# The last slice of the last tile scaled on the scalar engine and stored from its own queue, the slice ahead of it on VectorE

## The chip, the cores and the metric

The kernel runs on one core of a Trainium2 chip. The metric is the device time of one execution in microseconds.

Some terms: a *semaphore* is a counter by which engines and stores tell each other that something is done, and an *event* is a moment at which one is raised. A store is *issued* from the queue of an engine, which is held meanwhile; in the traces it then raises its semaphore sixteen times, and the last of these events is its *landing*. The *exit* is what the program still does after the last landing.

## The reference, cut to what matters

Spatially reduced attention over 4 x 12288 queries of 128 channels is followed by a gated feed-forward network with 1536 hidden channels.

```python
def _moe_ref(x, w_gate, w_val, w_out):
    gate = np.maximum(x @ w_gate, 0.0)
    val = x @ w_val
    return (gate * val @ w_out).astype(np.float32)     # 49152 rows of 128 channels
```

The rows are worked off in 96 tiles of 512. The change touches the last of them alone, after its last matrix product: the values lie in PSUM, have to be multiplied by a constant, and have to be stored to memory.

## The kernel before

```python
    def out_scale(k, engine, own, o_ps=None):
        ...                                  # o_sb: three buffers used in turn
        if engine is nc.scalar:
            nc.scalar.mul(o_sb, o_ps, 1.0 / X_SCALE**2)
        else:
            nc.vector.tensor_scalar(o_sb, o_ps, 1.0 / X_SCALE**2, None, op0=ALU.mult)

    def out_store(k, own):
        nc.sync.dma_start(out[...][:, own], o_sbs[k][:, own])     # address cut

    def out_last(k):
        parts = [bank([128, 2, 128]), bank([128, 1, 128]), bank([128, 1, 128])]
        owns = [slice(0, 2), slice(2, 3), slice(3, 4)]
        ...
        def keep(n, engine):
            out_scale(k, engine, owns[n], parts[n])
            out_store(k, owns[n])
        held = NFB - 1
        add(0, 0, held)                       # add: matmuls of one slice of 128 rows
        add(1, 0, held)
        add(2, 0, held - 4)
        add(0, held, NFB)
        add(1, held, NFB)
        keep(0, nc.vector)                    # slices 0 and 1
        add(2, held - 4, NFB)
        keep(1, nc.scalar)                    # slice 2
        add(3, 0, NFB)
        keep(2, nc.vector)                    # slice 3: the last work of the kernel
```

In the main loop, the last two tiles ahead of this one are stored whole, also from the sync queue: `out_scale(kO, nc.vector, slice(0, NS)); out_store(kO, slice(0, NS))` and the same on ScalarE just before `out_last`.

The softmax here doesn't subtract the row's maximum and nothing guards it: scores larger than these inputs give would overflow.

Of the kernel before, what the change touches and what calls it, by code (L numbers as in the profile page):

```python
# [16 lines left out]
def kernel(  # L17
# [23 lines left out]
    nc = tc.nc  # L41
# [27 lines left out]
    def bank(shape, dtype=FP32):  # L69
        return psum.tile(shape, dtype, tag="bank", name="bank_ps")  # L70
# [228 lines left out]
    def out_add(k, fb, s, o_ps, first):  # L299
        nc.tensor.matmul(  # L300
            o_ps, hTs[k][:, fb, s * 128 : (s + 1) * 128], wo16[:, fb, :],
            start=first, stop=(fb == NFB - 1), skip_group_check=True,
        )
# [44 lines left out]
    def out_scale(k, engine, own, o_ps=None):  # L348
        if k not in o_sbs:
            o_sbs[k] = work.tile([128, NS, 128], FP32, tag="o_sb", bufs=3, name="o_sb")  # L350
        o_sb, o_ps = o_sbs[k][:, own], o_ps if o_ps is not None else o_banks[k]
        if engine is nc.scalar:
            nc.scalar.mul(o_sb, o_ps, 1.0 / X_SCALE**2)
        else:
            nc.vector.tensor_scalar(o_sb, o_ps, 1.0 / X_SCALE**2, None, op0=ALU.mult)

    def out_store(k, own):
        nc.sync.dma_start(
            out[k // GRP * GRP * T : (k // GRP + 1) * GRP * T, :].rearrange(
                "(p i s) c -> i p s c", p=128, i=GRP  # L360
            )[k % GRP][:, own], o_sbs[k][:, own],
        )
        if own.stop == NS:
            for tiles in (hTs, o_banks, o_sbs):
                del tiles[k]
# [4 lines that stand above are left out]
        o_banks[k] = None  # L370

        def add(s, fb0, fb1):
            n = max(s - 1, 0)
            for fb in range(fb0, fb1):
                out_add(k, fb, s, parts[n][:, s - owns[n].start], fb == 0 and s != 1)

        def keep(n, engine):
            out_scale(k, engine, owns[n], parts[n])
            out_store(k, owns[n])

        held = NFB - 1
        add(0, 0, held)
# [3 lines that stand above are left out]
        add(1, held, NFB)  # L386
        keep(0, nc.vector)
        add(2, held - 4, NFB)
        keep(1, nc.scalar)
        add(3, 0, NFB)  # L390
        keep(2, nc.vector)

    ctx.enter_context(tc.manual_schedule())

# [138 lines left out]
    for k in range(LAG, last + 1):  # L533
# [6 lines left out]
        for step in range(NFB):  # L540
            kO, kF = k - LAG - 1, k - LAG
            half, i = divmod(step // 2, NJC // 2)
            if 0 <= kO:
                out_proj(kO, step)
                if step == NFB - 1 and kO < NT - 3:
                    out_moves = out_turn(kO)
                elif step == NFB - 1 and k < last:
                    out_scale(kO, nc.vector, slice(0, NS))
                    out_store(kO, slice(0, NS))
# [41 lines left out]
            if b < B:  # L591
# [13 lines left out]
                if 0 <= pair < NJC // 2 and not odd and step == 1:  # L605
                    turn_values_dma(b, pair)
    out_scale(last - LAG - 1, nc.scalar, slice(0, NS))
    out_store(last - LAG - 1, slice(0, NS))
    out_last(last - LAG)


# [28 lines left out]
```

## Time and profile before

| | |
|---|---|
| time, median of the 6 runs beside the result | 1033.86 us (1033.05 to 1034.48) |
| span in the profile | 1031.32 us |
| TensorE busy | 1023.6 us, 99% |
| last matmul's semaphore event | 1027.94 us |
| **tail: from that event to the end of the span** | **3.379 us** |

The lines behind this are in the prediction. The tail is the quantity to follow: all that the change touches lies in it or just ahead of it. It is made of five steps, each read from the trace's records to the nanosecond: the event to the start of the last scale, the scale, its end to the start of the store's issue, issue to the last landing event, and from there to the end.

### The profile page before, as it was taken

What the parts mean: (1) busy time and instruction counts of PE and PEld (TensorE: products, weight loads), DVE (VectorE), ACT (ScalarE), POOL (GpSimd) and SP (SyncE); (2) the same over time, 40 slices, a digit from 0 to 9 for tenths busy, and PEclk for the clock granted to TensorE, in tenths of its full rate; (3) what the DMA queues carried; (4) which work ended last, traced back from release to release, by engine and by line L of the source; (5) the groups of instructions that cost most, each with busy time, mean ns of one, the idle gap of its engine ahead of it and who ended that gap; (6) DMA issues with size and microseconds to landing.
All of it is one profiled execution on the core that took longest, in us unless ns stands there. A gap on an engine that the chain in (4) does not pass through costs nothing.

```text
span 1031.3 us, 20034 instructions
## 1 busy us (share of the span) xinstructions
PE 1023.6 (99%) x6576; PEld 545.2 (53%) x6576; DVE 910.4 (88%) x1669; ACT 909.6 (88%) x1749; POOL 279.9 (27%) x287
## 2 busy tenths in 40 slices
PE   8999999999999999999999999999999999999998
PEld 5555555555555555555555555555555555555555
DVE  3889899998989898998889898989898888989898
ACT  4998888888988888888888889888888898888886
POOL 2212146521211124642212121664121221111110
PEclk9999999999999999999999999999999999999999
DMA  8836396452542547736345157573752434513122
GB/s 306 121 57 81 90 192 142 79 93 43 83 68 49 79 120 161 169 54 89 55 65 88 32 85 148 137 170 57 85 75 44 73 57 62 87 32 66 33 44 51
DMA packets 328824, 93.34 MB, mean 91 GB/s; under 512 B 308496, under 2 KB 321936, under 8 KB 328720
## 3 DMA queue, kind: packets, MB, share of 16 engines
q1 hardware_dynamic: 313632, 78.76, 38.7%
q0 software_dynamic: 14944, 13.24, 10.5%
q8 instruction: 51, 0.84, 0.3%
q14 instruction: 53, 0.43, 0.1%
q10 hardware_dynamic: 144, 0.07, 0.0%
HBM read 53.94 MB, written 26.35 MB: 78 GB/s over the span
## 4 chain that ended last, share of the span: by engine, by line
PE 98%; DMA 1%; ACT 0%; DVE 0%; SPq 0%; issue 0%
PE bank_ps L279 24%; PE bank_ps L290 24%; PE bank_ps L314 23%; PE bank_ps L241 13%; PE bank_ps L230 12%; DMA parts<-in_kv_dram 1%; PE bank_ps L300 1%; PE bank_ps L163 0%; PE bank_ps L189 0%; ACT aT L231 0%; DVE hT L293 0%; PE bank_ps L181 0%; SPq L139 0%; ACT kv L183 0%; PE bank_ps L119 0%
## 5 line engine op out<-in xcount | busy, mean ns | idle before, releaser
L293 DVE SCALAR_TENSOR_TENSOR hT<-bank_ps,val 128x512 f16<-128x512 f32 x1152 | 758.2, 687 | 91.6 <-ACT val L283 71.1
L283 ACT CAST val<-bank_ps 128x512 f16<-128x512 f32 x1152 | 678.7, 591 | 102.5 <-PE bank_ps L279 100.5
L279 PE MATMUL bank_ps<-xT,wv 128*128 128x512 f16 x1152 | 436.6, 379 | 0.1
L290 PE MATMUL bank_ps<-xT,wg 128*128 128x512 f16 x1152 | 436.6, 379 | 0.0
L314 PE MATMUL bank_ps<-hT,wo 128*128 128x512 f16 x1116 | 423.0, 379 | 0.0
L231 ACT ACTIVATE aT<-bank_ps 128x512 f16<-128x512 f32 x576 | 346.3, 605 | 0.9 <-PE bank_ps L230 0.8
L324 POOL TENSOR_SCALAR o_sb<-o_t 128x512 f32<-128x512 f32 x93 | 138.5, 1489 | 694.0 <-DVE rinv L249 684.1
L241 PEld LDWEIGHTS <-aT 128*128 128x128 f16 x2304 | 177.2, 98 | 133.4 <-issue 0.9
L241 PE MATMUL bank_ps<-kv,aT 128*128 128x129 f16 x2304 | 223.5, 220 | 0.5 <-DVE kv L199 0.4
L230 PE MATMUL bank_ps<-qT,kv 128*128 128x512 f16 x576 | 216.8, 379 | 0.4 <-DVE qT L122 0.2
L279 PEld LDWEIGHTS <-wv 128*128 128x128 f16 x1152 | 112.7, 98 | 132.2 <-issue 0.2
L290 PEld LDWEIGHTS <-wg 128*128 128x128 f16 x1152 | 112.7, 98 | 67.2 <-issue 0.2
L314 PEld LDWEIGHTS <-wo 128*128 128x128 f16 x1116 | 109.2, 98 | 65.9
L230 PEld LDWEIGHTS <-kv 128*128 128x128 f16 x576 | 56.1, 98 | 68.0 <-ACT kv L183 0.8
L257 DVE TENSOR_TENSOR x<-bank_ps,rinv 128x256 f16<-128x256 f32 x188 | 79.7, 425 | 6.6
L322 DVE STREAM_TRANSPOSE o_t<-bank_ps 128x512 f32<-128x512 f32 x93 | 65.7, 706 | 0.0
L86 POOL DMA_DIRECT2D q<-in_q_dram x88 | 48.4, 557 | 0.3 <-issue 0.3
L148 POOL TENSOR_TENSOR s<-parts 128x512 f32<-128x512 f32 x36 | 44.9, 1267 | 0.0
L249 DVE RECIPROCAL rinv<-bank_ps 128x2 f32<-128x2 f32 x192 | 28.0, 146 | 0.6 <-PE bank_ps L241 0.6
L150 POOL TENSOR_TENSOR s<-s 128x512 f32<-128x512 f32 x18 | 22.8, 1269 | 1.4
L152 POOL TENSOR_TENSOR c<-s 128x256 f32<-128x256 f32 x18 | 13.1, 728 | 1.4
L300 PEld LDWEIGHTS <-hT 128*128 128x128 f16 x144 | 10.1, 98 | 6.1 <-DVE hT L293 0.3
(53 smaller groups left out, 95.0 us busy)
## 6 DMA issues: line engine op xcount, KB each, us to landing
parts<-in_kv_dram SPq DMA_DIRECT2D x48, 512.0 KB, 6.6
out_dram<-o_sb SPq DMA_DIRECT2D x354, 64.0 KB, 2.2
q<-in_q_dram POOLq DMA_DIRECT2D x88, 128.0 KB, 4.4
xT<-x SPq DMA_TRANSPOSE x94, 2.5
out_dram<-o_sb SPq DMA_DIRECT2D x80, 16.0 KB, 1.5
placed<-blocks SPq DMA_DIRECT2D x9, 128.0 KB, 1.8
kvT<-placed SPq DMA_DIRECT2D x36, 32.0 KB, 2.0
q<-in_q_dram SPq DMA_DIRECT2D x2, 512.0 KB, 7.9
```

Source lines behind the costliest of these rows:

```text
L86: nc.gpsimd.dma_start(q16[32 * j : 32 * (j + 1)].rearrange("t (i s) c -> t i s c", i=GRP), rows[j])
L230: nc.tensor.matmul(s_ps, kv16[:, k // NST, jc, 0:C], qT_of(k), start=True, stop=True)
L231: nc.scalar.activation(aTs[k][:, jc, :], s_ps, AF.Exp, scale=qk_scale)
L241: nc.tensor.matmul(x_ps[:, i, :], aTs[k][:, jc, s * 128 : (s + 1) * 128], kv16[:, k // NST, jc, C : 2 * C + 1], start=(jc == 0 and i == 0) ...
L257: nc.vector.tensor_tensor(x16s[k][:, 2 * half : 2 * half + 2, :], x_ps[:, :, 0:C], rinv.to_broadcast([128, 2, C]), op=ALU.mult,)
L279: nc.tensor.matmul(va_ps, wv16[:, fb * 128 : (fb + 1) * 128], xTs[k], start=True, stop=True)
L283: nc.scalar.copy(val, va_ps)
L290: nc.tensor.matmul(g_ps, wg16[:, fb * 128 : (fb + 1) * 128], xTs[k], start=True, stop=True)
L293: nc.vector.scalar_tensor_tensor(hTs[k][:, fb, :], g_ps, 0.0, vals.pop((k, fb)), op0=ALU.max, op1=ALU.mult)
L314: nc.tensor.matmul(o_banks[k], wo16[:, fb, :], hTs[k][:, fb, :], start=fb == 0, stop=fb == NFB - 1)
L322: nc.vector.transpose(o_t, o_banks.pop(k))
L324: nc.gpsimd.tensor_scalar(o_sb.rearrange("t j s c -> t s j c"), o_t.rearrange("t (s j c) -> t s j c", s=NS, j=4), 1.0 / X_SCALE**2, None, ...
```

## The change

The intent is to give the last store an empty queue: the engine that scales the last slice also issues its store, and does not stand behind the two sync stores ahead. The slice ahead then goes to VectorE.

```diff
-    def out_store(k, own):
-        nc.sync.dma_start(
+    def out_store(k, own, queue=nc.sync):
+        queue.dma_start(
...
-        def keep(n, engine):
+        def keep(n, engine, queue=nc.sync):
             out_scale(k, engine, owns[n], parts[n])
-            out_store(k, owns[n])
+            out_store(k, owns[n], queue)
...
-        keep(1, nc.scalar)
+        keep(1, nc.vector)
         add(3, 0, NFB)
-        keep(2, nc.vector)
+        keep(2, nc.scalar, nc.scalar)
```

## The prediction

> **What bounds the kernel now.** I read the page first, for which engine fills the span and whether the end of the kernel can matter at all.
>
> ```profile
> span 1031.3 us, 20034 instructions
> PE 1023.6 (99%) x6576; PEld 545.2 (53%) x6576; DVE 910.4 (88%) x1669; ACT 909.6 (88%) x1749; POOL 279.9 (27%) x287
> PE 98%; DMA 1%; ACT 0%; DVE 0%; SPq 0%; issue 0%
> ```
>
> TensorE fills 99% of the span and 98% of the chain that ended last. The change touches no matmul. So whatever it does happens in the few microseconds after the last matmul. The chain in order of time, asked for the last 7 us, shows where that tail begins:
>
> ```profile
> 1025.63 2.31 PE bank_ps L300 x38
> 1027.94 0.02 issue
> 1027.96 0.29 DVE o_sb L355
> ```
>
> The last matmul releases VectorE at 1027.94. From there to the end of the span, 1031.3, are 3.36 us, 0.33% of the span. Even if all of it vanished, the result would be "within 2%". What is left to find is the sign and the tenths of a microsecond. The timeline of the tail, engine by engine (columns: start in us, duration in us, engine, line, operation):
>
> ```profile
> 1027.34 0.28 ACT L353 ACTIVATE o_sb<-bank_ps 128x128 f32<-128x128 f32 x1 [1.49 <-PE bank_ps L300]
> ...
> 1027.07 0.42 DVE L355 TENSOR_SCALAR o_sb<-bank_ps 128x256 f32<-128x256 f32 x1 [0.90 <-PE bank_ps L300]
> 1027.96 0.29 DVE L355 TENSOR_SCALAR o_sb<-bank_ps 128x128 f32<-128x128 f32 x1 [0.47 <-PE bank_ps L300]
> ...
> 1027.53 0.33 SPq L358 DMA_DIRECT2D out_dram<-o_sb  x1
> ...
> 1027.95 0.39 SPq L358 DMA_DIRECT2D out_dram<-o_sb  x1
> ...
> 1028.43 0.40 SPq L358 DMA_DIRECT2D out_dram<-o_sb  x1
> ```
>
> Three pieces of the last tile are scaled (slices 0-1 on VectorE, slice 2 on ScalarE, slice 3 on VectorE), and three stores leave one after another from the sync queue. The last scale ends at 1027.965 + 0.292 = 1028.257 (the trace's records to the ns), yet its store starts only at 1028.429. It waits for its queue, not for its data. The second store is issued until 1028.337, and a semaphore instruction stands between the two (1028.383, 17 ns). Where the queue was free, for the first store, the start came 28 ns after the scale's end (1027.499 to 1027.527). So 172 - 28 = 144 ns of the path to the end is the sync queue's own issuing. That is what the change can win.
>
> After the issue, the line's own view and the queue's waits give the rest:
>
> ```profile
> L358 SPq DMA_DIRECT2D out_dram<-o_sb x1: 397/397/397, 1028.4 to 1028.4; - x1
> DMA to landing us min/median/max: 1.7/1.7/1.7
> ...
> SPq L635 <- DMA out_dram<-o_sb: 1.1, 3, 0.5
> ```
>
> The last landing event is at 1030.150, 1.721 us after the issue began, and the exit (sync's remaining checks, then two rounds of all engines) runs to 1031.32, 1.17 us more. The wait at L635 is sync waiting for the last three landings in turn.
>
> **What the Trainium skill says.**
> 1. "DMA: Bandwidth & Descriptors", section "Issuing engines are not separate DMA queues": stores from different engines share the same 16 DMA engines, and issuing from several saves only the sequencer's issue time. The trace agrees that this time is what is at stake: an issue holds sync 0.33 to 0.40 us, the landing takes 1.7 to 1.9.
> 2. "Perfetto Trace Analysis", section "DMA Instruction — HWDGE (DVE, Sync)": the block that generates descriptors is shared between issuing sequencers and locked for one at a time. The trace has one hint: at the start, the one load from ScalarE's queue (0.732, 377 ns) lay beside the first load from sync (0.729), whose issue took 696 ns against about 600 for the next ones. That suggests sharing at a cost of some 0.1 us, not a full wait.
> 3. "ScalarE: Activation LUTs", section "What ACT_TABLE_LOAD costs": an ACTIVATE with immediate scale takes 186 ns plus 0.833 ns per element, so 293 ns at 128. The trace has 278 for just this shape, which I use.
>
> **The change, part by part.**
>
> *Slice 2 moves from ScalarE to VectorE.* It needs the matmuls of slice 2 (ScalarE began at 1027.343) and VectorE free of the first piece (1027.499). It runs about 1027.50 to 1027.50 + 0.29 = 1027.79, against 1027.62 now, 0.17 later. Its store cannot be issued by sync before 1027.952 in either kernel, since the first store holds the queue to 1027.859 and the semaphore instruction and dispatch add 93 ns. Slack 0.16 us; cost on the path: zero.
>
> *Slice 3 moves from VectorE to ScalarE.* The matmul's semaphore event is at 1027.941. VectorE started 24 ns after it because its older waits were already met. ScalarE in the present kernel started 72 ns after its event (1027.271 to 1027.343), because its wait is split: semaphore instructions ahead, then the operation. Those waits, on the earlier stores of the buffer, go with the first use of the new tile by an engine, so they will stand ahead of ScalarE's slice 3 too. Start 1027.941 + 0.072 = 1028.013. End + 0.278 = 1028.291, 34 ns later than VectorE's 1028.257 (48 lost at the start, 14 won in duration).
>
> *The last store moves to ScalarE's queue.* It is the only store there, so it starts about 28 ns after the scale: 1028.32 instead of 1028.429, which is 0.11 earlier. Sync issues the second store until 1028.337, so the two hardly overlap (about 20 ns). Landing: 1.72 us as now, or 1.79 as ScalarE's own load of the same 64 KB at the start (0.732 to its last landing event, 2.517):
>
> ```profile
> 0.73 0.38 ACTq L403 DMA_DIRECT2D w_sr_f<-in_w_sr_dram  x1
> ...
> w_sr_f<-in_w_sr_dram ACTq DMA_DIRECT2D x1, 64.0 KB, 1.8
> ```
>
> That gives 1030.04 to 1030.11 against 1030.150: a gain of 0.04 to 0.11 us.
>
> *The exit.* The semaphores of stores go round in program order over both queues (the trace shows the same one for ScalarE's load and for later sync stores). The last store therefore should keep its place in sync's list of final waits, and the exit its 1.17 us. The second store lands at 1029.758 as now, before the last one, so it does not become the end. ScalarE's closing drain comes earlier than sync's.
>
> Sum: 0.00 (slice 2) + 0.034 (slower start on ScalarE) - 0.144 (no queue ahead) + 0 to 0.07 (landing) = -0.11 to -0.04 us. The span goes from 1031.3 to about 1031.2, and the time from 1033.97 to 1033.9.
>
> **The rivals.**
>
> *The shared descriptor block makes the store from ScalarE wait or slows it.* For it: the skill's statement, and the 0.1 us longer issue of the first load. Also, first packets moved 0.997 us after the ScalarE issue began, against some 0.89 for the last sync stores (1028.429 to 1029.320). Against it: the overlap here is only about 20 ns. If the whole 0.1 applies, the gain is zero: 1033.95 to 1034.05.
>
> *The exit order changes.* If the new store were waited for last rather than in the middle, sync's four checks after it (each about 60 ns apart, 1030.167 to 1030.408) would be done before the landing, and another 0.2 us would go: 1033.65. Against it: the semaphores rotate as said. If ScalarE's queue brings one more check or drain: plus 0.06 to 0.1, 1034.0.
>
> *ScalarE is late for another reason.* Its waits on nine store semaphores could be met late. Against it: in the present kernel they run at 1024.8 to 1025.4 and the last stands idle for 1895 ns. The buffer's old stores have long landed. At most a tenth of a microsecond.
>
> **Range and chances.** All of these together span 1033.6 to 1034.1. The three runs before spread over 1033.8 to 1034.48, so run-to-run variation is larger than the whole effect. I widen to 1033.1 to 1034.6 for it and for another session. The middle is 1033.9. Reaching 2% would take 20.7 us, six times the whole tail: 0.99 within, half a per cent on either side for an accident I cannot see.
>
> **What would show it right or wrong.** Right: slice 2 on VectorE directly behind the first piece with the second sync issue still near 10 ns of its place relative to the last matmul; slice 3 on ScalarE starting some 70 ns after the last matmul's event and lasting 0.28; a store on ScalarE's queue starting about 0.38 us after that event (sync: 0.49 now); landing 1.7 to 1.8 us later; an exit of 1.17 us. Wrong steps: a second sync store that starts later; a ScalarE issue much over 0.40 us or a landing over 1.85 (contention); an exit of another length (wait order). The prediction itself would be wrong if the main loop moved, that is, if the last matmul's event shifted by microseconds, which nothing in this change should cause.

## The result, and the profile after

The changed kernel took 1033.53 us, median of 6 runs (1032.74 to 1034.25), against 1033.86 before. The ratio is 0.9997 with a 95% interval of 0.9984 to 1.001: the same. (A ratio is the mean time of one kernel's fast runs over that of the other's of the same rounds, so not quite the ratio of the medians quoted.) The times alone do not show that anything changed.

The profile does. First the page of the changed kernel:

```profile
span 1031.8 us, 20033 instructions
PE 1023.4 (99%) x6576; PEld 544.4 (53%) x6576; DVE 909.9 (88%) x1669; ACT 909.6 (88%) x1749; POOL 279.9 (27%) x287
PE 97%; DMA 1%; ACT 1%; DVE 0%; SPq 0%; issue 0%; ACTq 0%
```

The span of this one execution is 0.44 us longer than the one of before, although the changed part became shorter. The chain of the tail in order of time shows both:

```profile
1026.14 2.31 PE bank_ps L300 x38
1028.45 0.03 ACTq L353
1028.48 0.04 issue
1028.53 0.28 ACT o_sb L353
```

The last matmul's event came at 1028.454, 0.513 us later than in the profile before, because of work that the change does not touch (see "How much the rest of the kernel moves"). From there the chain goes to ScalarE now. The timeline of the changed kernel (start, duration, engine, line, operation):

```profile
1027.59 0.42 DVE L355 TENSOR_SCALAR o_sb<-bank_ps 128x256 f32<-128x256 f32 x1 [0.90 <-PE bank_ps L300]
1027.93 0.28 DVE L355 TENSOR_SCALAR o_sb<-bank_ps 128x128 f32<-128x128 f32 x1
...
1028.53 0.28 ACT L353 ACTIVATE o_sb<-bank_ps 128x128 f32<-128x128 f32 x1 [2.15 <-PE bank_ps L300]
1028.83 0.35 ACTq L358 DMA_DIRECT2D out_dram<-o_sb  x1
...
1028.04 0.33 SPq L358 DMA_DIRECT2D out_dram<-o_sb  x1
...
1028.46 0.38 SPq L358 DMA_DIRECT2D out_dram<-o_sb  x1
```

VectorE scales slice 2 directly behind the first piece; ScalarE scales slice 3 and issues its store 29 ns after the scale's end. Its issue overlaps that of the second sync store by 15 ns (1028.833 to 1028.848). What follows the issue:

```profile
L358 ACTq DMA_DIRECT2D out_dram<-o_sb x1: 353/353/353, 1028.8 to 1028.8; - x1
DMA to landing us min/median/max: 1.8/1.8/1.8
...
SPq L635 <- DMA out_dram<-o_sb: 1.5, 3, 1.0
```

The third line, from the queue's waits, was 1.1 us in total with 0.5 as the longest before: sync has one store less to issue, stands at its closing checks earlier and waits longer there. Longer waiting on an engine that has nothing else to do is not a loss. The five steps side by side, in ns:

| step | before | predicted | after | difference |
|---|---|---|---|---|
| event to scale | 24 | 72 | 72 | +48 |
| scale | 292 | 278 | 278 | -14 |
| scale to issue | 172 | 28 | 29 | -143 |
| issue to last landing | 1721 | 1721 to 1790 | 1753 | +32 |
| landing to end | 1170 | 1170 | 1170 | 0 |
| **tail** | **3379** | | **3302** | **-77** |

### The profile page after: what moved, and what is told of

Same layout as the page of the kernel before. It is cut to its first block, busy times and chain, and to the rows that moved or that the text cites. A ratio compares the mean times of both kernels' runs of the same rounds, so it can differ in the third digit from the quotient of the medians.

```text
span 1031.8 us, 20033 instructions
## 1 busy us (share of the span) xinstructions
PE 1023.4 (99%) x6576; PEld 544.4 (53%) x6576; DVE 909.9 (88%) x1669; ACT 909.6 (88%) x1749; POOL 279.9 (27%) x287
## 4 chain that ended last, share of the span: by engine, by line
PE 97%; DMA 1%; ACT 1%; DVE 0%; SPq 0%; issue 0%; ACTq 0%
PE bank_ps L279 24%; PE bank_ps L290 24%; PE bank_ps L314 23%; PE bank_ps L241 13%; PE bank_ps L230 12%; DMA xT<-x 1%; DMA parts<-in_kv_dram 1%; PE bank_ps L300 1%; PE bank_ps L163 0%; ACT aT L231 0%; PE bank_ps L189 0%; DVE hT L293 0%; PE bank_ps L181 0%; SPq L139 0%; ACT kv L183 0%
```

## The experiments

The theory: the gain is the sync queue's issue time, no longer in front of the last store. The exchange of engines gains nothing and costs the 48 ns at ScalarE's start. The rival: the exchange of engines is what helps. A second rival is chance. Nine kernels ran; all gave correct results. Each was profiled, and this is what the traces' records say, in ns after the last matmul's event (its place in the span, in us, is in the second column). "Store ahead" is the last landing event of the store before the last.

| run | event, us | scale start | scale end | issue | store ahead landed | landed | tail |
|---|---|---|---|---|---|---|---|
| before | 1027.94 | 24 | 316 | 488 | 1817 | 2209 | 3379 |
| r_before | 1028.23 | 22 | 314 | 486 | 1806 | 2206 | 3376 |
| after | 1028.45 | 72 | 350 | 379 | 1801 | 2132 | 3302 |
| r_after | 1029.33 | 72 | 350 | 380 | 1800 | 2128 | 3298 |
| e1_swap_only | 1028.20 | 72 | 349 | 488 | 1790 | 2213 | 3383 |
| e2_queue_only | 1029.03 | 22 | 314 | 346 | 1801 | 2116 | 3286 |
| e3_both_scalar | 1028.60 | 23 | 300 | 330 | 1815 | 2116 | 3286 |
| e4_middle_store | 1028.09 | 23 | 314 | 342 | 1831 | 2081 | 3251 |
| e5_both_scalar_queue | 1028.33 | 23 | 315 | 347 | 1833 | 2088 | 3258 |
| e6_later_check | 1027.99 | 71 | 348 | 378 | 1885 | 2109 | 3037 |
| e7_middle_and_check | 1028.08 | 23 | 314 | 342 | 1895 | 2107 | 3036 |

### r_before and r_after: does the tail repeat?

No edit; the two kernels again.

> The kernel before, unchanged, profiled once more. Theory: the tail, from the last matmul's semaphore event to the end of the span, is fixed by instructions and transfers (3.379 us in the first profile) and repeats to about 0.02 us, while the event itself moves between executions by some tenths of a microsecond (1027.94 in the first profile of before, 1028.45 in that of after). Rival: the tail itself varies by as much as the 0.077 us between the two first profiles (3.379 and 3.302), and that difference says nothing.

> The changed kernel, profiled once more. Theory: tail 3.30 us within 0.02, made of 0.072 to the scale, 0.278 scale, 0.029 to the issue, 1.753 to the landing, 1.170 exit. Rival (chance): a tail anywhere between 3.25 and 3.40.

The tails were 3376 and 3298 ns, 3 and 4 ns from those of the first profiles, and every step within 5 ns. The event meanwhile moved by 0.29 and 0.87 us. So 77 ns is a real difference of the tail, twenty times its repeat error, and chance is out. These runs took 1033.39 us (before) and 1034.41 (changed); the order is the opposite of the result's, and again says nothing.

### e1_swap_only: the engines without the queue

Against the changed kernel:

```diff
-        keep(2, nc.scalar, nc.scalar)
+        keep(2, nc.scalar)
```

> Only the engines of the scales are swapped; all stores stay in the sync queue. Theory (the gain is the queue's): the scale on ScalarE ends 0.350 us after the last matmul's event, but the sync queue is ready for the third store only 0.488 after it, as before; tail 3.38 us, as before, although the scale ends 34 ns later. Rival (the gain comes from scaling on ScalarE, or from the slice ahead being on VectorE): tail 3.30.

```profile
1028.27 0.28 ACT L353 ACTIVATE o_sb<-bank_ps 128x128 f32<-128x128 f32 x1 [2.15 <-PE bank_ps L300]
...
1028.21 0.39 SPq L358 DMA_DIRECT2D out_dram<-o_sb  x1
...
1028.68 0.40 SPq L358 DMA_DIRECT2D out_dram<-o_sb  x1
```

The scale ended at 349, 33 ns later than before, and the issue came at 488 all the same. Between the scale's end (1028.55) and the last issue (1028.68) the queue is busy with the store ahead until 1028.59, then with its semaphore instruction. Tail 3383: the exchange alone is worth nothing, and the rival's 3.30 is excluded. This is also why the exchange costs nothing as long as the queue is the bound: of the 172 ns between scale and issue in the kernel before, 143 were waiting for the queue, and the 33 come out of these.

### e2_queue_only: the queue without the engines

Against the changed kernel:

```diff
-        keep(1, nc.vector)
+        keep(1, nc.scalar)
-        keep(2, nc.scalar, nc.scalar)
+        keep(2, nc.vector, nc.scalar)
```

> Only the last store's queue is changed to ScalarE's; the scales stay as in the kernel before (slice 2 ScalarE, slice 3 VectorE). Theory: scale starts 0.024 after the event, ends at 0.316, store issued from ScalarE at 0.344, landing 1.753 later, exit 1.170: tail 3.267 us, better than the full change by about 0.035, so that the swap of engines costs rather than helps. Rival (the store has to follow a scale on its own engine to be issued early; a wait across engines costs as much as the queue did): tail 3.30 or more.

```profile
1029.05 0.29 DVE L355 TENSOR_SCALAR o_sb<-bank_ps 128x128 f32<-128x128 f32 x1 [0.47 <-PE bank_ps L300]
...
1029.37 0.36 ACTq L358 DMA_DIRECT2D out_dram<-o_sb  x1
```

Tail 3286, so the queue alone gains 93 ns, 16 more than the full change. A store on ScalarE's queue can follow a scale on VectorE within 32 ns (314 to 346): having both on one engine is not needed. The issue was 33 ns earlier than in the full change, as expected, but the landing only 16 ns earlier. So half of what is gained at the issue is given back behind it, which my 3267 did not contain. The next three runs ask why.

### e3_both_scalar: where ScalarE's 48 ns come from

Against the changed kernel:

```diff
-        keep(1, nc.vector)
+        keep(1, nc.scalar)
```

> Slices 2 and 3 are both scaled on ScalarE, the last store leaves from its queue. Theory (ScalarE's 72 ns are the price of its first use of the tile's buffer, with the waits on old stores ahead of it): here slice 2 pays it, and slice 3 starts 0.024 after the last matmul's event, ends at 0.302 and its store is issued at 0.331. Rival (ScalarE simply answers TensorE later than VectorE does): start at 0.072, issue at 0.380 as in the full change. Landing: if it counts from the issue alone, 1.753, tail 3.254; if a store close behind another lands later, as the only-queue run suggested (1.770 at 0.346), then 1.775 to 1.79 and a tail of 3.275 to 3.29.

```profile
1028.00 0.28 ACT L353 ACTIVATE o_sb<-bank_ps 128x128 f32<-128x128 f32 x1 [1.48 <-PE bank_ps L300]
1028.62 0.28 ACT L353 ACTIVATE o_sb<-bank_ps 128x128 f32<-128x128 f32 x1 [0.34 <-PE bank_ps L300]
1028.93 0.35 ACTq L358 DMA_DIRECT2D out_dram<-o_sb  x1
```

With slice 2 ahead of it on the same engine, ScalarE answered the last event within 23 ns, as VectorE does. The 72 ns are the price of the engine's first use of the tile's buffer: its wait for TensorE stands in a separate semaphore instruction, together with the last of the waits on old stores, and the scale follows only after that. VectorE pays it too: in the kernel before, its first use of this buffer, the scale of slices 0 and 1, began 82 ns after the event that it waited for (1026.992 to 1027.074). The issue came 49 ns earlier than in the full change, and the landing 16 ns earlier: still more was given back.

### e4_middle_store and e5_both_scalar_queue: closeness, or ScalarE's queue?

e4, against the kernel before (with the `queue` argument of the change):

```diff
-        keep(1, nc.scalar)
+        keep(1, nc.scalar, nc.scalar)
```

e5, against e4:

```diff
-        keep(2, nc.vector)
+        keep(2, nc.vector, nc.scalar)
```

> As the kernel before, but the middle store (slice 2), not the last, leaves from ScalarE's queue. Theory: sync is free long before the last scale ends (0.314 after the event), so it issues the last store at 0.344; the middle store is issued from ScalarE at about -0.29, while sync is still issuing the first store (-0.416 to -0.084). The last store then follows its neighbour by 0.63 us instead of 0.34, and lands 1.72 after its issue, as in the kernel before: tail 3.235. Rival (the block that makes descriptors is shared, so that two issues at once cost a full issue time): the middle store's issue takes 0.5 us or more, or its packets start over 1.1 us after its issue instead of 0.87, and the first store's issue grows beyond 0.333.

> As the run with the middle store on ScalarE's queue, but the last store leaves from ScalarE's queue too; its distance to the store ahead is the same. Tells two explanations of the slower landing (1.75 to 1.77 against 1.72 in sync's queue) apart. Closeness to the store ahead: here they are 0.63 us apart, so 1.72, tail 3.235. ScalarE's queue itself: 1.75 to 1.77, tail 3.27 to 3.29.

The timeline of e4, and its line view of the first two stores:

```profile
1027.80 0.35 ACTq L358 DMA_DIRECT2D out_dram<-o_sb  x1
...
1027.68 0.33 SPq L358 DMA_DIRECT2D out_dram<-o_sb  x1
...
1028.44 0.33 SPq L358 DMA_DIRECT2D out_dram<-o_sb  x1
```

```profile
L358 SPq DMA_DIRECT2D out_dram<-o_sb x1: 333/333/333, 1027.7 to 1027.7; - x1
L358 ACTq DMA_DIRECT2D out_dram<-o_sb x1: 354/354/354, 1027.8 to 1027.8; - x1
...
DMA to landing us min/median/max: 2.0/2.1/2.1
```

The last store took 1739 ns to land from the sync queue (e4) and 1741 from ScalarE's (e5), at the same distance to the store ahead. ScalarE's queue is therefore not slower. My other explanation, closeness, fits three runs only: at 0.37, 0.34 and 0.32 us behind its neighbour (after, e2, e3) the store took 1753, 1770 and 1786. In the kernel before it took 1721 at 0.48 us, less than e4 at 0.63; e6 at 0.36 took 1731, and e7 at 0.63 took 1765. So the distance of the issues does not decide it.

The DMA packets in the traces show where the time is lost. From the issue to the end of the store's last packet it is 1195 to 1263 ns in all eleven profiles, and not longer after an early issue (before 1245, after 1220, e2 1229, e3 1226, e4 1195). From the last packet to the landing it is 462 to 476 ns in before, r_before and e1, and 499 to 566 in the others (after 533, e2 541, e3 560, e4 544). No packet moves in this time. In e4, for the stretch in which the first two stores meet and for the one from the last packet to the landing, the view of `--windows` has (the last two numbers are the DMA share and GB/s)

```profile
1028.67:1028.87 0.20, 0.00 (x0) 0.00 (x0) 0.00 (x0) 0.00 (x0) 0.00 (x0) 1.00 0.97 340
...
1029.63:1030.18 0.55, 0.00 (x0) 0.00 (x0) 0.00 (x0) 0.00 (x0) 0.00 (x0) 1.00 0.00 0
```

So what an early issue gives back is lost behind the packets, where only the completion events are still to come. The sixteen landing events of the last store come about 12 ns apart (closer in e6 and e7), and in every run the first of them comes after the last of the store ahead. The gap between the two stores' last events shrinks from 392 ns (before) to 331, 315 and 301 (after, e2, e3), to about 250 (e4, e5), and to 224 and 212 (e6, e7). An earlier issue gains less as the landings close up. Why one store's events stay behind the other's, these runs do not tell.

e4 also tests the rival in its sharp form. Two issues overlapped for 210 ns (1027.803 to 1028.013) and took 333 and 354 ns, as they do alone (332 and 353): neither sequencer waited. Yet the middle store's packets started 1075 ns after its issue, against 868 for the last store of the changed kernel, and both overlapping stores landed after 2.04 and 2.12 us instead of 1.78 to 1.90. The trace shows something that they shared: the DMA engines. With 868 ns the middle store's packets would have begun 577 ns after the last matmul's event (an estimate, -291 + 868); but from 575 to 775 ns sixteen packets of the first store were under way at every point sampled, 25 ns apart (the share of 0.97 above). The middle store's first packet moved at 784 ns, when the first store's first closing packet of 4 bytes (777 to 785) was ending. A wait for busy DMA engines accounts for the 0.2 us; a loss in the descriptor block is neither needed for it nor excluded for a part of it. Here it lies beside the last matmuls and costs nothing.

### e6_later_check: the closing checks

Against the changed kernel:

```diff
-                    out_store(kO, slice(0, NS))
+                    for s in range(NS):
+                        out_store(kO, slice(s, s + 1))
...
-    out_store(last - LAG - 1, slice(0, NS))
+    out_store(last - LAG - 1, slice(0, 2))
+    out_store(last - LAG - 1, slice(2, NS))
```

> The full change, and the stores of the two tiles ahead are cut into four and two pieces, so that four more stores are issued off the path and the last one gets the last of the eight semaphores that go round. Theory: sync checks the eight one after another, some 61 ns each, and in the kernels so far four checks come after the one that the last landing ends; here they are done before it, so the exit is 1.170 - 0.245 = 0.925 us and the tail about 3.06. Rival (the exit is fixed by the rounds of all engines, not by sync's checks): exit 1.17, tail 3.30.

The line view of the closing instructions, from the last landing on, in the changed kernel:

```profile
L635 SPq EVENT_SEMAPHORE  x5: 28/28/28, 1030.6 to 1030.8; - x5
L635 SPq DRAIN  x2: 7/10/13, 1030.9 to 1031.0; - x2
```

and in e6 (where two added lines shift the number):

```profile
L637 SPq DRAIN  x2: 7/10/13, 1030.2 to 1030.3; - x2
L637 SPq EVENT_SEMAPHORE  x1: 28/28/28, 1030.1 to 1030.1; - x1
```

Five checks after the landing became one. They stand about 61 ns apart (1030.602, 1030.662, 1030.723, 1030.782, 1030.844 in the changed kernel), and the exit went from 1170 to 928 ns. The tail is 3037, 265 below the changed kernel's: 242 from the exit, 23 from an earlier landing. Cutting stores that have time to spare thus brought over three times the gain of the change itself. The rival of a fixed exit is out.

### e7_middle_and_check: the best of both

e4 with the stores cut as in e6.

> The two things that shortened the tail most, together: the middle store from ScalarE's queue (tail 3.251 alone) and the last store on the last of the eight semaphores (exit 0.928 instead of 1.170). Theory: they add, so tail 3.251 - 0.242 = 3.01 us, 0.37 shorter than before. Rival: stores of the tiles ahead, now six, crowd the last ones and give back some, tail 3.1. On the time both kernels should differ by 0.04%, which five rounds, with runs that spread over 1 us and more, should not resolve: ratio between 0.998 and 1.002, verdict same.

The tail is 3036 ns, 343 below the kernel before, but 1 ns from e6: the earlier issue of e4 is worth nothing here. Its last store was issued 36 ns earlier than in e6 and landed 2 ns earlier. The store ahead landed at 1895, and 212 ns after that is the closest of all runs; that the one holds back the other is likely, not shown. The expected 3010 was 26 ns too low. In time, over five rounds, it took 1033.23 us in the median against 1033.77 of the kernel before, ratio 0.9995 with an interval of 0.9981 to 1.0009: the same, as the sizes demand.

### How much the rest of the kernel moves

The event's place varied from 1027.94 to 1029.33 over the profiles. Comparing the start of each matmul with the first profile, the difference arises almost wholly in two places (e6 has a third, 0.17 us at 183 us). One is the first 25 us, where the first loads land: -0.13 to 0.66 us. The other is one matmul at about 687 us, which in some executions waits for a transposed tile. In r_after, this matmul's line in the timeline is

```profile
687.92 0.39 PE L279 MATMUL bank_ps<-xT,wv 128*128 128x512 f16 x1 [0.65 <-DMA xT<-x]
```

and it put that execution 0.81 us behind the first profile, in which there is no such wait. Its place in the code is the same in all kernels, and it came in executions of both (r_before 0.42 us, after 0.34, r_after 0.81, e2 0.90, e5 0.52, e7 0.26; none in before, e1, e3, e4 and e6). This variation, ten times the 77 ns, is why the times cannot show the change. The prediction named a shift of the event by microseconds as a sign that it was wrong; in r_after the event came 1.39 us later than in the first profile of before, and these two places account for it. What makes the transpose late there was not examined.

## Why the prediction was right

Within 2% was forecast at 0.99, because the whole tail is 0.33% of the span. The ratio of 0.9997 agrees, and the median of 1033.53 us lies in the range of 1033.1 to 1034.6. The middle, 1033.9, was 0.4 us too high; the shift of the tail accounts for 0.08 us of the medians' 0.33, and the rest is within the variation of the loop.

**Slice 2 on VectorE: zero cost, shown.** VectorE overlapped the two scales a little, so slice 2 ended 245 ns before the event, earlier than my estimate of 151 before it; the second sync issue kept its place (10 ns after the event against 11).

**ScalarE's late start: 72 ns, shown.** The step was read from ScalarE's first use of the buffer in the kernel before, and came out to the nanosecond. e3 confirmed the reason given: on its second use the start is 23 ns. One detail was misread: of the nine semaphores in those waits eight are the stores', and the ninth is TensorE's.

**The queue ahead: 144 ns, shown.** 143 were gained, and e1 and e2 separate it from the exchange of engines: the exchange alone gains nothing (3383), the queue alone more than both together (3286).

**The landing: 1.72 to 1.79 us, the size right, the reason not.** It took 1753 ns. I had put the upper end down to ScalarE's queue, from its load at the start. e4 and e5 show that the queue is not slower. The packets were done 1220 ns after the issue, sooner than before (1245); the completion events came 533 ns behind them instead of 476. That this fell inside the range was in part luck.

**The exit and the order of the checks: shown.** The last store kept its semaphore (the same number in both traces), and the exit is 1170 ns in both. The rival of a changed order was rightly refused for this change; e6 shows that its size, 0.2 us, was right as well (242 ns).

**The rival of the shared block** was rightly held small: the 15 ns of overlap in the change cost no visible wait. Even e4's 210 ns lengthened neither issue, and the 0.2 us by which packets came later go with busy DMA engines. The hint of the first load (696 ns) was weak too: a later load issued from sync alone took 867 ns (at 5.09 us).

So the sum, -0.11 to -0.04 us, met the measured -0.077 with each of its terms, the landing's for another reason than the one given.

## What to carry to other kernels

Before judging a change at the end of a kernel, measure the tail from the last matmul's event: it repeats to some nanoseconds where the time varies by a microsecond, and it also bounds what can be won. Here a second queue brought the last issue forward by 109 to 158 ns, and 77 to 128 of these reached the end. With the closing checks as they were it gave the most to the store of the middle (128); with the checks moved (e7 against e6) that was worth 1 ns. Changing the engine that computes gained nothing by itself (e1) and cost 16 ns beside the new queue (after against e2). Then look behind the last landing: cutting earlier stores, so that the last one was checked last, brought over three times as much here as moving the store.

## What the Trainium skill lacked or had wrong

- "Perfetto Trace Analysis", section "DMA Instruction — HWDGE (DVE, Sync)", puts the wait for the shared descriptor block inside the profiled issue. No run here shows such a wait: two issues that overlapped for 210 ns took 333 and 354 ns, as alone (332 and 353). That does not prove the page wrong, since the profile does not show when an issue holds the block.
- "DMA: Bandwidth & Descriptors", section "Issuing engines are not separate DMA queues", is right that issue time is what is saved (143 ns here). The page has no figure for how much of an earlier issue arrives at the landing: of 109 ns here 77, since the time from the last packet to the landing grew from 476 to 533 ns; and the last store never landed less than 212 ns after the store ahead.
- "ScalarE: Activation LUTs", section "What ACT_TABLE_LOAD costs": 186 ns plus 0.833 ns per element gives 293 ns for 128 elements; the profiles here show 277 to 278, and VectorE's 291 to 292 for the same shape alone.
- No page that I read has the closing checks of the stores' semaphores: about 61 ns each, one after another, so that the place of the last store among eight decides 242 ns of the exit (1170 or 928).
- None of these pages has the price of an engine's first use of a recycled buffer behind a split wait: 72 ns from the last matmul's event to the scale, against 22 to 24 on a later use (VectorE's own first use: 82 ns).
